# Output projection moved into the head loop, and V 30 and V 31 loaded in smaller pieces

## The chip, the cores and the metric

One core of a Trainium2 chip runs the whole program. The metric is the device time of one execution in microseconds (us); a profiled execution also gives a span, from the first to the last instruction, which is about 2 us shorter (1292.4 against 1294.16 us in the profiled execution of the kernel before). A time is the median of several executions; a profile shows one of them.

Engines: in this kernel PE does matmuls, DVE and ACT do vector and scalar work, POOL a few small things, SP issues nearly all DMA transfers. The DMA share on the profile's page is a mean over the core's 16 DMA engines. SBUF and PSUM are the core's on-chip memories; this kernel has PE write its results to PSUM. A load is counted as landed at the 16th increment of its semaphore. The granted clock is the share of PE's full clock that the profile records as granted; in the records it is 0.5 or 1.

## The reference, cut to what matters

One decode step of an attention block and an MLP. The caches are 32 heads x 32768 keys x 128 in bf16: 268 MB of K and 268 MB of V, each byte used once.

```python
def _A_ref(x, k_cache, v_cache, wq, wo):          # B = Sq = 1, D = 512, H = 32, Sk = 32768, Dh = 128
    q = (x @ wq).reshape(B, Sq, H, Dh).transpose(0, 2, 1, 3)
    scores = jnp.einsum("bhqd,bhkd->bhqk", q, k_cache) * (Dh ** -0.5)
    p = softmax(scores)
    o = jnp.einsum("bhqk,bhkd->bhqd", p, v_cache)
    return o.transpose(0, 2, 1, 3).reshape(B, Sq, H * Dh) @ wo
h  = x + _A_ref(layernorm(x), ...)
h2 = h + mish_mlp(layernorm(h))                   # 512 -> 1376 -> 512
```

## The kernel before

A head is 32 groups of 1024 keys. In each group PE transposes K into PSUM (`tps`), DVE copies the result to SBUF (`kt`), PE forms scores (`sps`), and PE forms the V product (`ops`) of a group 40 groups back. V 31 is the V of head 31, K 31 its K. PE runs heads 2 to 31 as a hardware loop; all other engines run straight-line code. K and V use two halves of one ring; V 31, the last V, goes into the K half.

Each load is one DMA issued by SP in a fixed order (`pos`), after what it overwrites was used (`after`). A normal load is half a head, 4 MB, with 32 KB per partition; 128 in the list below means 4 MB, and 32 means 1 MB (8 KB per partition).

```python
LAST_K = [128, 32, 32, 32, 32]
LAST_V = [128, 64, 32, 16, 8, 8]
# ...
for j, n in enumerate(sizes):
    g1 = g + n // 8
    if kind == "k":
        after = [f"trb{(h - 1) * GH + g1 - 1}"] if h else []
        pos, count = h * GH + g, h
    else:
        after = [f"pv{(h - 1) * GH + g1 - 1}"] if h else ...
        if own:                                   # V 31
            after = [f"trb{h * GH + g1 - 1}"]
        pos, count = (h + 1) * GH + LAG + g + 0.5, h + 1
# ...
```

The output projection runs after the loop, between the groups of the last V product: 31 products of one row, four matmuls (the profile shows 8, L649) that fold the row into columns, and row sums `wbar` of wo.

```python
def y_row(h):
    p = 32 * (h % 4)
    S.step(PE, lambda: t_.matmul(yrow[p:p + 1, :], oT[:, h:h + 1], wo_sb[:, h, :], ...),
           waits=[f"oT{h}", ("wo", 16)], name=f"yr{h}")
# ... after the loop:
for t in range(GH):
    group(H, t)                                   # ends V 30, begins V 31
    if t == 1:
        y_init()
        for h in range(H - 2, H):
            w_bar(h)
        # ...
    if 2 <= t < 8:
        for h in range((H - 2) * (t - 2) // 6, (H - 2) * (t - 1) // 6):
            y_row(h)
    # ...
```

The copy is this one, 1024 times in a run:

```python
def evac(i):
    # ...
    dve(i, lambda: v.tensor_copy(kt[:, i % NE, :], T_b[i % 2][:, :]), f"ev{i}", waits)
```

Of the kernel before, what the change touches and what calls it, by code (L numbers as in the profile page):

```python
# [19 lines left out]
LAST_K = [128, 32, 32, 32, 32]  # L20
LAST_V = [128, 64, 32, 16, 8, 8]

# [10 lines left out]
class _Sched:  # L33
# [5 lines left out]
    def __init__(self, nc, emit, events, sems, only=None):  # L39
        self.nc = nc  # L40
        self.emit = emit
        self.only = only
        self.ev = events
        self.sems = sems
        self.cnt = {}
        self.waited = {}
        self.taken = {}
        self.skip = False
        self.log = []
        self.engines = None  # L50
        if emit:
            self.engines = {PE: nc.tensor, ACT: nc.scalar, DVE: nc.vector, POOL: nc.gpsimd, SP: nc.sync}
# [66 lines left out]
    def repeat(self, rounds, body):  # L119

        if not self.emit or self.only != PE:
            for r in rounds:
                body(r)
            return
        first = None
        for r in rounds:
            self.waited, self.log = {}, []
            if r == rounds[0]:
                with self.nc.Fori(0, len(rounds), 1, engines=[mybir.EngineType.PE],
                                  head_slot={mybir.EngineType.PE: 0}):  # L130
                    body(r)
                first = self.log
                self.skip = True
            else:
                body(r)
                assert self.log == first, r
        self.skip = False
        self.waited = {}
# [27 lines left out]
def plan_loads(H, GH):  # L166


    NH = GH * 8 // PIECE
    loads = []  # L170
    for h in range(H):
        for kind in "kv":
            own = h == 0 if kind == "k" else h == H - 1
            sizes = (FIRST_K if kind == "k" else LAST_V) if own else [PIECE] * NH
            if kind == "k" and h == H - 1:
                sizes = LAST_K
            assert sum(sizes) == GH * 8 and max(sizes) <= PIECE
            g = 0
# [6 lines that stand above are left out]
                    after = [f"pv{(h - 1) * GH + g1 - 1}"] if h else ["q_done"] if g1 > GH // 2 else []  # L185
                    if own:
                        after = [f"trb{h * GH + g1 - 1}"]
                    pos, count = (h + 1) * GH + LAG + g + 0.5, h + 1
                chan = f"{kind}own{j}" if own else f"{kind}{j}"
                if kind == "k" and h == H - 1 and j >= NH - 1:  # L190
                    after = after + ["kx_off"]
                if j >= NH and not own:
                    chan, count = f"kx{j - NH}", 1
                loads.append(_Load(kind, h, g, g1, pos, chan, 16 if own else 16 * count, after))
                g = g1
    loads.sort(key=lambda x: x.pos)
    return loads


def build_kernel(nc, A_x, A_k_cache, A_v_cache, A_wq, A_wo, B_w1, B_b1, B_w2, out, NE=4):  # L200
# [33 lines left out]
    ring = sb([128, 2 * GH * R * 128], BF16, "ring")  # L234
    wo_sb = sb([128, H, D], BF16, "wo_sb")
    w1v = sb([128, KC, F], BF16, "w1_sb")
# [17 lines left out]
    qT = sb([128, 32], BF16, "qT")  # L254
    oT = sb([128, 32], BF16, "oT")
    qcur = sb([128, 2], BF16, "qcur")
    nb = sb([128, 1], F32, "nbias")
# [10 lines left out]
    yrs = sb([128, D], F32, "yrs")  # L268
    pscr = sb([1, 1], F32, "pscr")
    FP = FJ + FJ % 2  # L270
# [19 lines left out]
    Q0 = 160  # L290
    YC = yps[:, 0:KC * WIDE:WIDE]
    HROW = 128
# [43 lines left out]
    def program(S):  # L336
# [54 lines left out]
        for x in range(NX):  # L391
            S.dma(POOL, lambda x=x: g_.sem_inc(sems[f"kx{x}"], 16))

# [7 lines left out]
            b1r[FJ - 1:FJ, 0:FLAST], B_b1[(FJ - 1) * 128:F].rearrange("(o m) -> o m", o=1)).then_inc(sems["b1"], 16))  # L401
        for x in range(NX):
            S.dma(POOL, lambda x=x: g_.sem_inc(sems[f"kx{x}"], -16), waits=[f"trb{NK - GH - 1}"])
        S.step(POOL, lambda: g_.memset(pscr[:, :], 0.0), name="kx_off")
        S.step(DVE, lambda: v.memset(onesm[:, :], 1.0 / D))
# [4 lines left out]
        S.step(DVE, lambda: v.memset(onesf[:, :], 1.0))  # L410
        S.step(DVE, lambda: v.memset(yps[:, :], 0.0))
        S.step(DVE, lambda: v.memset(yrow[:, :], 0.0), name="consts")

# [82 lines left out]
        def values(i):  # L496
# [8 lines left out]
            if ld:  # L505
                waits.append((ld.chan, ld.count))
                if h < H - 1:
                    take[1] = (ld.chan, 16)
            for r in range(R):
                c = g * R + r  # L510
# [5 lines left out]
        def y_cols(h):  # L516
            waits = [f"oT{h}", ("wo", 16)]
            for c in range(KC):
                S.step(PE, lambda c=c: t_.matmul(
                    yps[:, c * WIDE:(c + 1) * WIDE], wo_sb[:, h, c * 128:(c + 1) * 128],  # L520
                    oT[:, h:h + 1].to_broadcast([128, WIDE]),
                    start=False, stop=(h == H - 1), skip_group_check=True), waits=(waits if c == 0 else ()),
                    name=(f"yc{h}" if c == KC - 1 else None))

        def y_row(h):
            p = 32 * (h % 4)
            S.step(PE, lambda: t_.matmul(  # L527
                yrow[p:p + 1, :], oT[:, h:h + 1], wo_sb[:, h, :], start=(h < 4), stop=(h >= H - 5),
                skip_group_check=True), waits=[f"oT{h}", ("wo", 16)], name=f"yr{h}")

        def y_init():
            for c in range(KC):
                S.step(PE, lambda c=c: t_.matmul(
                    yps[:, c * WIDE:(c + 1) * WIDE], xrow[0:1, c * 128:(c + 1) * 128],
                    oneb[0:1, 0:1].to_broadcast([1, WIDE]),
                    start=(c == 0), stop=False, skip_group_check=True),
                    waits=(["consts", ("xr", 16)] if c == 0 else ()))

# [3 lines left out]
        def group(hk, t):  # L542
# [52 lines left out]
            if 0 <= ho < H:  # L595
                if t == 2:
                    S.step(DVE, lambda: v.tensor_scalar_mul(o1s[:, ho:ho + 1], o_b[0][:, 0:1], rtot[:, ho:ho + 1]),  # L597
                           name=f"o1s{ho}", waits=[f"pv{ho * GH + GH - LAG - 1}", f"rcp{ho}"])
                elif t == LAG + 1:
                    add_o(ho)  # L600
                elif t == GH // 2 + 8 and ho < H - 2:
                    w_bar(ho)

        def add_o(ho):
            dve(LAG + 1, lambda: v.scalar_tensor_tensor(  # L605
                oT[:, ho:ho + 1], o_b[1][:, 0:1], rtot[:, ho:ho + 1], o1s[:, ho:ho + 1], ALU.mult, ALU.add),
                f"oT{ho}", [f"pv{ho * GH + GH - 1}", f"o1s{ho}"])

# [8 lines left out]
        def whole(hk):  # L617
            for t in range(GH):
                group(hk, t)

        S.repeat(range(2, H), whole)


        hl = H - 1
        for t in range(GH):
            group(H, t)
            if t == 1:
                y_init()
                for h in range(H - 2, H):
# [5 lines left out]
                    waits=["wbh0"])  # L635
            if 2 <= t < 8:
                for h in range((H - 2) * (t - 2) // 6, (H - 2) * (t - 1) // 6):
                    y_row(h)
            if t == LAG + 2:
                y_row(H - 2)  # L640
                S.step(DVE, lambda: v.tensor_tensor(wbo[:, 0:hl], wbar[:, 0:hl], oT[:, 0:hl], ALU.mult), name="wbo",
                       waits=[f"yr{H - 2}"])
                S.step(DVE, lambda: v.tensor_reduce(wbs[:, :], wbo[:, 0:hl], AXX, ALU.add), name="wbs", waits=["wbo"])
                S.step(DVE, lambda: v.tensor_copy(yrs[:, :], yrow[:, :]), name="yrs")
            if t == LAG + 6:
                S.step(PE, lambda: t_.matmul(YM, onesm[:, :], wbs[:, :], start=False, stop=False, skip_group_check=True),
                       waits=["wbs"])
                for c in range(KC):
                    S.step(PE, lambda c=c: t_.matmul(  # L649
                        yps[:, c * WIDE:c * WIDE + 1], yrs[:, c * 128:(c + 1) * 128], onesf[:, 0:1],  # L650
                        start=False, stop=False, skip_group_check=True), waits=(["yrs"] if c == 0 else ()))
                S.step(PE, lambda: t_.matmul(T_b[0][:, 0:FP], b1r[:, :], identb[0:FP, 0:FP],
# [104 lines left out]
```

## Time and profile before

| | before |
|---|---|
| time, median of the 3 runs | 1295.8 us |
| span of the profiled execution | 1292.4 us |
| last K piece lands | 1263.14 us |
| last V piece lands | 1282.88 us |
| V product ends (PE) | 1284.02 us |
| output copy starts | 1289.97 us |

The landings are read from the trace's semaphore records. These lines are from the profile's page of the kernel before: busy time per engine, the busy tenths of the DMA engines and their GB/s in 40 slices of the span, and the DMA queues (packets, MB, share of 16 engines' span).

```profile
PE 1028.1 (80%) x25114; PEld 994.3 (77%) x25114; DVE 776.2 (60%) x1379; ACT 34.0 (3%) x134; POOL 2.6 (0%) x11
...
DMA  9999999999999999999999999999999999999997
GB/s 373 424 411 425 430 431 429 436 430 430 433 428 435 433 428 433 428 435 433 428 435 429 432 434 427 432 433 429 433 431 430 426 427 434 427 434 428 431 405 285
...
q1 hardware_dynamic: 27816, 548.09, 99.4%
q8 instruction: 20, 0.33, 0.1%
q14 instruction: 13, 0.11, 0.0%
```

The mean over the 16 DMA engines is at 9 tenths or more up to the last slice.

The chain of waits of the kernel before, its end (start us, us, what; followed back from the last instruction):

```profile
1277.72 4.81 PE ops L511 x181
1282.52 0.86 issue
1283.38 0.65 PE ops L511 x19
...
1284.06 0.23 DVE oT L605
...
1285.24 0.73 PE sps L676 x24
1285.98 0.22 PE hlp L683 x2
1286.20 0.73 PE sps L676 x20
...
1288.58 1.37 PE yps L707 x44
...
1289.97 0.29 DVE outsb L711
```

PE works through the groups of V 31 without a wait for data and ends 1.14 us after the last landing. PE is behind here, not DMA; the 0.86 us called issue is a stall in the middle of a group, where no wait stands. The last instruction fetch before it (16 KB, on the queue q8) began at 1280.82 us and took 1.05 us.

Two lines of the timeline before (start us, us, engine, line, operation, count, and the idle time before it with what ended it):

```profile
1260.70 0.36 PE L511 MATMUL ops<-pbuf,ring 128*128 128x32 bf16 x8 [3.10 <-DMA ring<-in_A_v_cache_dram]
...
1283.38 0.64 PE L511 MATMUL ops<-pbuf,ring 128*128 128x32 bf16 x19 [0.86 <-issue]
```

The first is PE's wait for the second half of V 30, 3.1 us.

### The profile page before, as it was taken

How to read it: one execution, taken by the hardware profiler on the slowest of the kernel's cores; microseconds unless marked ns; L12 is line 12 of the kernel's file. 1: busy time of each engine (PE TensorE's matmuls, PEld its weight loads, DVE VectorE, ACT ScalarE, POOL GpSimd, SP SyncE). 2: the span in 40 equal slices, each digit the busy share in tenths (PEclk: the TensorE clock that was granted, in tenths of full speed). 3: DMA queues.
4: the chain of work that ended last, by engine and by line, in shares of the span. 5: the costliest groups of instructions: out<-in, count | busy, mean ns of one | idle time of the engine just before them, and what ended most of it. 6: DMA issues, size and time to landing. Idle time of an engine off the chain costs nothing.

```text
span 1292.4 us, 52224 instructions
## 1 busy us (share of the span) xinstructions
PE 1028.1 (80%) x25114; PEld 994.3 (77%) x25114; DVE 776.2 (60%) x1379; ACT 34.0 (3%) x134; POOL 2.6 (0%) x11
## 2 busy tenths in 40 slices
PE   6757877787787788787787787887877877878888
PEld 6757877787787787787787777887877877877876
DVE  5635566565666565565565665665655655655663
ACT  0000000000000000000000000000000000000000
POOL 0000000000000000000000000000000000000000
PEclk9868888998988998988998988988998888988988
DMA  9999999999999999999999999999999999999997
GB/s 373 424 411 425 430 431 429 436 430 430 433 428 435 433 428 433 428 435 433 428 435 429 432 434 427 432 433 429 433 431 430 426 427 434 427 434 428 431 405 285
DMA packets 27945, 548.53 MB, mean 424 GB/s; under 512 B 2600, under 2 KB 9608, under 8 KB 10888
## 3 DMA queue, kind: packets, MB, share of 16 engines
q1 hardware_dynamic: 27816, 548.09, 99.4%
q8 instruction: 20, 0.33, 0.1%
q14 instruction: 13, 0.11, 0.0%
q0 software_dynamic: 96, 0.00, 0.0%
HBM read 548.08 MB, written 0.00 MB: 424 GB/s over the span
## 4 chain that ended last, share of the span: by engine, by line
DMA 63%; PE 33%; DVE 3%; issue 0%; SPq 0%; ACT 0%
DMA ring<-in_A_k_cache_dram 50%; PE tps L470 17%; DMA ring<-in_A_v_cache_dram 14%; PE ops L511 7%; PE sps L491 6%; DVE kt L479 1%; PE hlp L581 1%; DVE scb L563 1%; DVE pmax L561 1%; PE hlp L565 1%; PE hlp L569 1%; PE yrow L527 0%; SPq L352 0%; PE sps L676 0%; PE yps L707 0%
## 5 line engine op out<-in xcount | busy, mean ns | idle before, releaser
L479 DVE COPY kt<-tps 128x1024 bf16<-128x1024 bf16 x1024 | 707.5, 692 | 487.2 <-PE tps L470 480.1
L470 PE MATMUL tps<-identb,ring 128*128 128x128 bf16 x8192 | 695.8, 234 | 192.7 <-DMA ring<-in_A_k_cache_dram 191.5
L470 PEld LDWEIGHTS tps<-identb,ring 128*128 128x128 bf16 x8192 | 523.3, 104 | 199.7 <-DMA ring<-in_A_k_cache_dram 198.5
L511 PE MATMUL ops<-pbuf,ring 128*128 128x32 bf16 x8192 | 361.2, 178 | 51.6 <-DMA ring<-in_A_v_cache_dram 50.3
L491 PE MATMUL sps<-qcur,kt 128*128 128x32 bf16 x8192 | 376.0, 180 | 8.2 <-DVE scb L563 6.8
L491 PEld LDWEIGHTS sps<-qcur,kt 128*128 128x128 bf16 x8192 | 328.7, 99 | 16.2 <-DVE scb L563 14.4
L511 PEld LDWEIGHTS ops<-pbuf,ring 128*128 128x128 bf16 x8192 | 281.3, 97 | 65.8 <-DMA ring<-in_A_v_cache_dram 50.1
L572 ACT ACTIVATE pbuf<-scb,nbias 128x192 bf16<-128x192 f32 x32 | 14.6, 456 | 1174.5 <-PE ops L511 1100.1
L610 DVE TENSOR_REDUCE wbar<-wo_sb 128x1 f32<-128x512 bf16 x32 | 21.6, 676 | 0.0
L581 PE MATMUL hlp<-esum,onesf 128*128 128x1 f32 x128 | 18.7, 250 | 0.0
L581 PEld LDWEIGHTS hlp<-esum,onesf 128*128 128x128 f32 x128 | 16.7, 190 | 0.2 <-issue 0.2
L561 DVE TENSOR_REDUCE pmax<-sps 128x1 f32<-128x256 f32 x32 | 13.3, 415 | 0.5 <-PE sps L491 0.5
L563 DVE COPY scb<-sps 128x256 f32<-128x256 f32 x32 | 13.2, 414 | 0.0
L565 PE MATMUL hlp<-ident,pmax 128*1 128x128 f32 x64 | 13.1, 290 | 0.0
L576 ACT ACTIVATE pbuf<-scb,nbias 128x64 bf16<-128x64 f32 x32 | 11.2, 348 | 62.1 <-PE ops L511 62.1
L569 PE MATMUL hlp<-gmax,onesr 1*128 1x1 f32 x64 | 12.1, 256 | 0.5 <-DVE gmax L567 0.5
L569 PEld LDWEIGHTS hlp<-gmax,onesr 1*128 1x128 f32 x64 | 9.4, 182 | 2.0 <-DVE gmax L567 1.0
L605 DVE SCALAR_TENSOR_TENSOR oT<-ops,rtot,o1s 128x1 bf16<-128x1 f32 x32 | 6.8, 212 | 5.1 <-PE ops L511 5.1
L597 DVE TENSOR_SCALAR o1s<-ops,rtot 128x1 f32<-128x1 f32 x32 | 6.7, 209 | 3.4 <-PE ops L511 3.4
L567 DVE TENSOR_REDUCE gmax<-hlp 1x1 f32<-1x128 f32 x32 | 8.7, 271 | 0.1
L576 ACT ACTIVATION_READ_ACCUMULATOR pbuf<-scb,nbias 128x1 f32 x32 | 6.0, 187 | 0.0
L572 ACT ACTIVATION_READ_ACCUMULATOR pbuf<-scb,nbias 128x1 f32 x32 | 6.0, 186 | 0.0
(87 smaller groups left out, 60.1 us busy)
## 6 DMA issues: line engine op xcount, KB each, us to landing
ring<-in_A_v_cache_dram SPq DMA_DIRECT2D x63, 4096.0 KB, 20.9
ring<-in_A_k_cache_dram SPq DMA_DIRECT2D x62, 4096.0 KB, 23.1
ring<-in_A_k_cache_dram SPq DMA_DIRECT2D x5, 1024.0 KB, 17.6
wo_sb<-in_A_wo_dram SPq DMA_DIRECT2D x1, 4096.0 KB, 37.7
ring<-in_A_wq_dram SPq DMA_DIRECT2D x1, 3584.0 KB, 30.6
ring<-in_A_k_cache_dram SPq DMA_DIRECT2D x1, 2048.0 KB, 12.3
ring<-in_A_v_cache_dram SPq DMA_DIRECT2D x1, 2048.0 KB, 21.2
ring<-in_A_v_cache_dram SPq DMA_DIRECT2D x1, 1024.0 KB, 17.1
```

The costliest lines, as they stand in the source:

```text
L470: S.step(PE, lambda r=r: t_.matmul(tb[:, r * 128:(r + 1) * 128], block("k", i, r), identb[:, :], is_transpose=True, start=True, stop=True) ...
L479: dve(i, lambda: v.tensor_copy(kt[:, i % NE, :], T_b[i % 2][:, :]), f"ev{i}", waits)
L491: S.step(PE, lambda r=r, c=c: t_.matmul(S_b[:, c:c + WIDE], kt[:, i % NE, r * 128:(r + 1) * 128], q.to_broadcast([128, WIDE]), start=True, ...
L511: S.step(PE, lambda r=r, c=c: t_.matmul(ob[:, 0:WIDE], block("v", i, r), pbuf[:, c:c + 1].to_broadcast([128, WIDE]), start=(r == 0 and g i ...
L561: dve(i, lambda: v.tensor_reduce(pmax[:, :], S_b[:, 0:NCOL], AXX, ALU.max), f"pmax{hs}", [f"qkb{hs * GH + GH - 1}"])
L563: dve(i, lambda: v.tensor_copy(scb[:, :], S_b[:, 0:NCOL]), f"sc{hs}", [])
L565: S.step(PE, lambda: t_.matmul(A_REG, pmax[:, :], ident[:, :], start=True, stop=True), name=f"A{hs}", waits=[f"pmax{hs}"] + (["qT" if H > ...
L569: S.step(PE, lambda: t_.matmul(B_REG, onesr[0:1, :], gmax[0:1, :], start=True, stop=True), name=f"B{hs}", waits=[f"gmax{hs}"])
L572: S.step(ACT, lambda: a.activation(pbuf[:, 0:CV], scb[:, 0:CV], ACTF.Exp, bias=nb[:, :], scale=SC, accum_out=esum[:, 0:1]), name=f"exp{hs} ...
L576: S.step(ACT, lambda: a.activation(pbuf[:, CV:NCOL], scb[:, CV:NCOL], ACTF.Exp, bias=nb[:, :], scale=SC, accum_out=esum[:, 1:2]), name=f"e ...
L581: S.step(PE, lambda s=s: t_.matmul(C_REG, onesf[:, :], esum[:, s:s + 1], start=(s == 0), stop=(s == 1)), name=(f"C{hs}" if s else None), w ...
L610: S.step(DVE, lambda: v.tensor_reduce(wbar[:, h:h + 1], wo_sb[:, h, :], AXX, ALU.add), waits=[("wo", 16)], name=f"wbar{h}")
```

## The change

The intent: take PE work out of the tail (the projection's row products go into the loop, one per head, with wo addressed by the loop's register), and let PE begin V 30's second half and V 31's first half earlier, by loading them in 1 MB pieces. Because PE's loop has one code for all heads, the extra V pieces get semaphores `vx` that stand at 16 in all other heads, as `kx` already did for K 31.

```diff
-LAST_V = [128, 64, 32, 16, 8, 8]
+LAST_V = [32, 32, 32, 32, 64, 32, 16, 8, 8]
...
-            if kind == "k" and h == H - 1:
+            if (kind, h) in (("k", H - 1), ("v", H - 2)):
                 sizes = LAST_K
...
-                if kind == "k" and h == H - 1 and j >= NH - 1:
-                    after = after + ["kx_off"]
+                if (kind, h) in (("k", H - 1), ("v", H - 2)) and j >= NH - 1:
+                    after = after + [f"{kind}x_off"]
...
         def y_row(h):
-            p = 32 * (h % 4)
+            rhs = wo_sb[:, h, :] if S.round is None else wo_flat[:, bass.ds(S.round * D, D)]
             S.step(PE, lambda: t_.matmul(
-                yrow[p:p + 1, :], oT[:, h:h + 1], wo_sb[:, h, :], start=(h < 4), stop=(h >= H - 5),
-                skip_group_check=True), waits=[f"oT{h}", ("wo", 16)], name=f"yr{h}")
+                yrow[:, :], ocur[:, 0:1].to_broadcast([128, 128]), rhs, start=False, stop=(h == H - 2),
+                skip_group_check=True), waits=[f"oc{h}"], name=f"yr{h}")
...
                 elif t == LAG + 1:
+                    if ho < H - 1:
+                        dve(LAG + 1, lambda: v.scalar_tensor_tensor(
+                            ocur[:, :], o_b[1][:, 0:1], rtot[:, ho:ho + 1], o1s[:, ho:ho + 1], ALU.mult, ALU.add), ...)
                     add_o(ho)
+                elif t == LAG + 4 and ho < H - 1:
+                    y_row(ho)
...
-            if 2 <= t < 8:
-                for h in range((H - 2) * (t - 2) // 6, (H - 2) * (t - 1) // 6):
-                    y_row(h)
...
-                for c in range(KC):                      # fold the row into columns by 4 matmuls
-                    ...
+                for c in range(KC):                      # or: mask with the identity on DVE, reduce, 1 matmul
+                    S.step(DVE, lambda c=c: v.tensor_tensor(
+                        yrs[:, c * 128:(c + 1) * 128], yrow[:, c * 128:(c + 1) * 128], ident[:, :], ALU.mult), ...)
...
```

The row sums of wo for heads 30 and 31 also move, from t = 1 (in front of the last softmax on DVE) to t = LAG.

More of the change, by code (lines that the diff above doesn't have):

```diff
@@ L49, in __init__ @@
         self.log = []
+        self.round = None
         self.engines = None
@@ L129, in repeat @@
                 with self.nc.Fori(0, len(rounds), 1, engines=[mybir.EngineType.PE],
-                                  head_slot={mybir.EngineType.PE: 0}):
+                                  head_slot={mybir.EngineType.PE: 0}) as i:
+                    self.round = i
                     body(r)
                 first = self.log
+                self.round = None
                 self.skip = True
@@ L189, in plan_loads @@
                 chan = f"{kind}own{j}" if own else f"{kind}{j}"
-                if kind == "k" and h == H - 1 and j >= NH - 1:
-                    after = after + ["kx_off"]
+                if (kind, h) in (("k", H - 1), ("v", H - 2)) and j >= NH - 1:
+                    after = after + [f"{kind}x_off"]
                 if j >= NH and not own:
-                    chan, count = f"kx{j - NH}", 1
+                    chan, count = f"{kind}x{j - NH}", 1
                 loads.append(_Load(kind, h, g, g1, pos, chan, 16 if own else 16 * count, after))
@@ L234, in build_kernel @@
     ring = sb([128, 2 * GH * R * 128], BF16, "ring")
-    wo_sb = sb([128, H, D], BF16, "wo_sb")
+    wo_flat = sb([128, H * D], BF16, "wo_sb")
+    wo_sb = wo_flat.rearrange("p (h n) -> p h n", h=H)
     w1v = sb([128, KC, F], BF16, "w1_sb")
@@ L255, in build_kernel @@
     oT = sb([128, 32], BF16, "oT")
+    ocur = sb([128, 1], BF16, "ocur")
     qcur = sb([128, 2], BF16, "qcur")
@@ L268, in build_kernel @@
     yrs = sb([128, D], F32, "yrs")
-    pscr = sb([1, 1], F32, "pscr")
+    ycol = sb([128, KC], F32, "ycol")
+    pscr = sb([1, 2], F32, "pscr")
     FP = FJ + FJ % 2
@@ L290, in build_kernel @@
     Q0 = 160
-    YC = yps[:, 0:KC * WIDE:WIDE]
+    YC = yps[:, 0:KC]
     HROW = 128
@@ L391, in program @@
         for x in range(NX):
-            S.dma(POOL, lambda x=x: g_.sem_inc(sems[f"kx{x}"], 16))
+            for k in "kv":
+                S.dma(POOL, lambda x=x, k=k: g_.sem_inc(sems[f"{k}x{x}"], 16))
         S.step(POOL, lambda: g_.iota(identi[:, :], [[-1, 128]], base=0, channel_multiplier=1), name="iota")
@@ L401, in program @@
             b1r[FJ - 1:FJ, 0:FLAST], B_b1[(FJ - 1) * 128:F].rearrange("(o m) -> o m", o=1)).then_inc(sems["b1"], 16))
-        for x in range(NX):
-            S.dma(POOL, lambda x=x: g_.sem_inc(sems[f"kx{x}"], -16), waits=[f"trb{NK - GH - 1}"])
-        S.step(POOL, lambda: g_.memset(pscr[:, :], 0.0), name="kx_off")
+        for k, done in (("k", f"trb{NK - GH - 1}"), ("v", f"pv{NK - 2 * GH - 1}")):
+            for x in range(NX):
+                S.dma(POOL, lambda x=x, k=k: g_.sem_inc(sems[f"{k}x{x}"], -16), waits=[done])
+            S.step(POOL, lambda: g_.memset(pscr[:, "kv".index(k):"kv".index(k) + 1], 0.0), name=f"{k}x_off")
         S.step(DVE, lambda: v.memset(onesm[:, :], 1.0 / D))
@@ L410, in program @@
         S.step(DVE, lambda: v.memset(onesf[:, :], 1.0))
-        S.step(DVE, lambda: v.memset(yps[:, :], 0.0))
-        S.step(DVE, lambda: v.memset(yrow[:, :], 0.0), name="consts")
+        S.step(DVE, lambda: v.memset(yps[:, :], 0.0), name="consts")
         S.step(ACT, lambda: a.preload_act_table_set("natural_log_exp_and_others"), count=False)
@@ L505, in values @@
             if ld:
-                waits.append((ld.chan, ld.count))
-                if h < H - 1:
+                if ld.chan[1] != "x":
+                    waits.append((ld.chan, ld.count))
+                if h < H - 1 and ld.chan[1] != "x":
                     take[1] = (ld.chan, 16)
+            if h < H - 1:
+                if g == GH // 2:
+                    for x in range(NX):
+                        take[2 + x] = (f"vx{x}", -16)
+                elif g in XG:
+                    x = XG.index(g)
+                    waits.append((f"vx{x}", 16))
+                    take[1] = (f"vx{x}", 16)
             for r in range(R):
@@ L519, in y_cols @@
                 S.step(PE, lambda c=c: t_.matmul(
-                    yps[:, c * WIDE:(c + 1) * WIDE], wo_sb[:, h, c * 128:(c + 1) * 128],
-                    oT[:, h:h + 1].to_broadcast([128, WIDE]),
+                    yps[:, c:c + 1], wo_sb[:, h, c * 128:(c + 1) * 128], oT[:, h:h + 1],
                     start=False, stop=(h == H - 1), skip_group_check=True), waits=(waits if c == 0 else ()),
@@ L525, in y_row @@
         def y_row(h):
-            p = 32 * (h % 4)
+            rhs = wo_sb[:, h, :] if S.round is None else wo_flat[:, bass.ds(S.round * D, D)]
             S.step(PE, lambda: t_.matmul(
-                yrow[p:p + 1, :], oT[:, h:h + 1], wo_sb[:, h, :], start=(h < 4), stop=(h >= H - 5),
-                skip_group_check=True), waits=[f"oT{h}", ("wo", 16)], name=f"yr{h}")
+                yrow[:, :], ocur[:, 0:1].to_broadcast([128, 128]), rhs, start=False, stop=(h == H - 2),
+                skip_group_check=True), waits=[f"oc{h}"], name=f"yr{h}")
         def y_init():
-            for c in range(KC):
-                S.step(PE, lambda c=c: t_.matmul(
-                    yps[:, c * WIDE:(c + 1) * WIDE], xrow[0:1, c * 128:(c + 1) * 128],
-                    oneb[0:1, 0:1].to_broadcast([1, WIDE]),
-                    start=(c == 0), stop=False, skip_group_check=True),
-                    waits=(["consts", ("xr", 16)] if c == 0 else ()))
+            S.step(PE, lambda: t_.matmul(
+                yrow[:, :], oneb[0:1, 0:1].to_broadcast([1, 128]), xrow[0:1, :], start=True, stop=False,
+                skip_group_check=True), waits=["consts", ("xr", 16), ("wo", 16)])
         CV = (GH - LAG) * R
@@ L599, in group @@
                 elif t == LAG + 1:
+                    if ho < H - 1:
+                        dve(LAG + 1, lambda: v.scalar_tensor_tensor(
+                            ocur[:, :], o_b[1][:, 0:1], rtot[:, ho:ho + 1], o1s[:, ho:ho + 1], ALU.mult, ALU.add),
+                            f"oc{ho}", [f"pv{ho * GH + GH - 1}", f"o1s{ho}"] + ([f"yr{ho - 1}"] if ho else []))
                     add_o(ho)
+                elif t == LAG + 4 and ho < H - 1:
+                    y_row(ho)
                 elif t == GH // 2 + 8 and ho < H - 2:
@@ L604, in add_o @@
         def add_o(ho):
-            dve(LAG + 1, lambda: v.scalar_tensor_tensor(
+            S.step(DVE, lambda: v.scalar_tensor_tensor(
                 oT[:, ho:ho + 1], o_b[1][:, 0:1], rtot[:, ho:ho + 1], o1s[:, ho:ho + 1], ALU.mult, ALU.add),
-                f"oT{ho}", [f"pv{ho * GH + GH - 1}", f"o1s{ho}"])
+                name=f"oT{ho}", waits=[f"pv{ho * GH + GH - 1}", f"o1s{ho}"])
         def w_bar(h):
@@ L619, in whole @@
                 group(hk, t)
+        y_init()
         S.repeat(range(2, H), whole)
@@ L626, in program @@
             group(H, t)
-            if t == 1:
-                y_init()
+            if t == LAG:
                 for h in range(H - 2, H):
@@ L635, in program @@
                     waits=["wbh0"])
-            if 2 <= t < 8:
-                for h in range((H - 2) * (t - 2) // 6, (H - 2) * (t - 1) // 6):
-                    y_row(h)
-            if t == LAG + 2:
-                y_row(H - 2)
+            if t == LAG + 5:
                 S.step(DVE, lambda: v.tensor_tensor(wbo[:, 0:hl], wbar[:, 0:hl], oT[:, 0:hl], ALU.mult), name="wbo",
-                       waits=[f"yr{H - 2}"])
+                       waits=[f"wbar{hl - 1}", f"oT{hl - 1}"])
                 S.step(DVE, lambda: v.tensor_reduce(wbs[:, :], wbo[:, 0:hl], AXX, ALU.add), name="wbs", waits=["wbo"])
-                S.step(DVE, lambda: v.tensor_copy(yrs[:, :], yrow[:, :]), name="yrs")
-            if t == LAG + 6:
+                for c in range(KC):
+                    S.step(DVE, lambda c=c: v.tensor_tensor(
+                        yrs[:, c * 128:(c + 1) * 128], yrow[:, c * 128:(c + 1) * 128], ident[:, :], ALU.mult),
+                        waits=[f"yr{hl - 1}"], name=(f"yrs" if c == KC - 1 else None))
+                S.step(DVE, lambda: v.tensor_reduce(
+                    ycol[:, :], yrs[:, :].rearrange("p (c n) -> p c n", c=KC), AXX, ALU.add), name="ycol", waits=["yrs"])
+            if t == LAG + 9:
+                S.step(PE, lambda: t_.matmul(YC, ident[:, :], ycol[:, :], start=True, stop=False,
+                                             skip_group_check=True), waits=["ycol"])
                 S.step(PE, lambda: t_.matmul(YM, onesm[:, :], wbs[:, :], start=False, stop=False, skip_group_check=True),
                        waits=["wbs"])
-                for c in range(KC):
-                    S.step(PE, lambda c=c: t_.matmul(
-                        yps[:, c * WIDE:c * WIDE + 1], yrs[:, c * 128:(c + 1) * 128], onesf[:, 0:1],
-                        start=False, stop=False, skip_group_check=True), waits=(["yrs"] if c == 0 else ()))
                 S.step(PE, lambda: t_.matmul(T_b[0][:, 0:FP], b1r[:, :], identb[0:FP, 0:FP],
```

## The prediction

> **What bounds it now.** The DMA queue, from start to the last V piece. The page's slices give a DMA busy share of 9 tenths or more up to the last slice. In the trace's record of loads landing, one 4 MB load lands every 9.71 us (432 GB/s) for the whole loop. [...] PE (80% busy) and DVE (60%) do not bind in the loop.
>
> At the end the landings are still back to back: second half of V 30 at 1260.65 us, last quarter of K 31 at 1263.14, pieces of V 31 at 1272.86, 1277.80, 1280.36, 1281.62, 1282.23, 1282.88. From 1250.95 to 1282.88, 13.6 MB take 31.9 us, against 31.6 at 432 GB/s. So no order of loads can bring the last V in much before 1282.9. The timeline shows what follows: PE ends its V product at 1284.03, the FFN chain ends with the output copy at 1290.26. In the weights' landings, the last w2 piece comes at 1288.62.
>
> **What the change does, costed.**
> - Removes from the tail 31 row products (groups of five take 0.52 us on the chain of waits: about 3.2 us), eight products that fold the row into columns (0.89), and moves two row sums of wo (1.27 on DVE) out of the last softmax. Adds there four masked products, one reduction, two small matmuls. In the loop: one 128x512 matmul and one 0.21 us DVE operation per head, plus a register offset: free, as PE has slack there.
> - V 30's second half as four 1 MB pieces: all four wait for the same event as the one load did (V 29 finished, 1242.97 us) plus a POOL step. But the first now lands about 1253.4 instead of 1260.65, and K 31's last quarter about 1255.8 instead of 1263.14. That removes PE's 3.1 us wait at 1257.6 (timeline), and K 31 ends about 3 us earlier. Pieces of 1 MB cost nothing: K 31's land 2.43 us apart, 432 GB/s.
> - V 31's first half in quarters lands its first rows about 7 us earlier, the last at the same time.
>
> So PE gets ahead in the tail, but then waits for V 31's last pieces. **On the critical path** remains only what PE was behind at the end: 1284.03 minus (1282.88 + one last group of 8 matmuls, 0.21, plus about 0.1 latency), i.e. 0.8 us. Part of that 0.8 is the 0.86 us stall of PE at 1282.52, which the profile calls issue and which follows an instruction fetch; it may fall elsewhere in the new tail.
>
> **Prediction.** The span falls by about 0.8 us, from 1292.4 to 1291.6; time 1294.9 us, range 1293.2 to 1296.6. Chances: faster by over 2% 0.01, within 2% 0.98, slower by over 2% 0.01.
>
> **What would show it.** Right: last V landing still near 1282.9; no PE wait of 3 us for V 30; PE gaps for V in the last 10 us; V product ended about 0.3 us after the last landing; loads still 9.71 us apart in the loop. Wrong: the last V lands over 1 us earlier or later, or PE is still working off a backlog then.
>
> **What would make it wrong.** About every 118 us one load takes some 1 us longer (10.7 instead of 9.7), mostly beside a small instruction fetch: one more or fewer moves the result as much as the change. PE, now waiting, may run the last chain at the lower granted clock (0.50 occurs after waits). The 0.86 us fetch stall may land inside the FFN chain. More pieces may cost some 0.05 us each.

The sum: 1284.03 - 1282.88 - 0.21 - 0.1 = 0.84, so 0.8 us. The 0.1 us of latency is the author's estimate; the trace of before has 0.05 us from a landing (1260.65) to the first matmul that uses it (1260.70). The 0.05 us per piece is an estimate too: K 31's last piece took 2.49 us against 2.43. "0.50 occurs after waits" can be seen in the clock record of before: in the 3.41 us before each of its 62 falls to 0.50, PE is busy 32% of the time in the median, against 80% over the run.

## More of the kernel before

The two queues named instruction move 0.44 MB of 548.

## The result, and the profile after

Ratios here and below are the mean time of one kernel's runs over that of the other's in the same rounds, so not quite the ratio of the medians.

| | before | after |
|---|---|---|
| time, median (4 runs each) | 1295.1 us | 1294.39 us |
| ratio to before, 95% interval | | 0.9994 (0.9976 to 1.0011) |
| span of the profiled execution | 1292.4 us | 1292.5 us |
| last K piece lands | 1263.14 us | 1255.91 us |
| last V piece lands | 1282.88 us | 1283.46 us |
| V product ends | 1284.02 us | 1283.91 us |
| output copy starts | 1289.97 us | 1290.15 us |

The page of the kernel after, the same lines:

```profile
PE 1030.9 (80%) x25105; PEld 995.3 (77%) x25105; DVE 777.5 (60%) x1413; ACT 33.9 (3%) x134; POOL 2.7 (0%) x12
...
DMA  9999999999999999999999999999999999999997
GB/s 373 424 410 423 434 432 428 435 430 430 436 427 434 431 431 433 428 434 432 430 433 429 432 434 429 433 429 424 431 431 430 435 427 434 432 430 428 431 382 305
...
q1 hardware_dynamic: 28680, 548.09, 99.3%
q8 instruction: 20, 0.33, 0.1%
q14 instruction: 13, 0.11, 0.0%
```

The chain of waits after, its end:

```profile
1264.62 18.84 DMA ring<-in_A_v_cache_dram
1283.46 0.05 issue
1283.51 0.41 PE ops L527 x8
...
1283.94 0.23 DVE oT L625
...
1285.15 0.78 PE sps L696 x24
1285.93 0.43 PE hlp L703 x2
1286.36 0.76 PE sps L696 x20
...
1288.76 1.37 PE yps L727 x44
...
1290.15 0.29 DVE outsb L731
```

And PE's waits in the timeline after:

```profile
1278.27 1.89 PE L527 MATMUL ops<-pbuf,ring 128*128 128x32 bf16 x64 [3.92 <-DMA ring<-in_A_v_cache_dram]
...
1280.76 1.04 PE L527 MATMUL ops<-pbuf,ring 128*128 128x32 bf16 x32 [0.59 <-DMA ring<-in_A_v_cache_dram]
...
1282.04 1.10 PE L527 MATMUL ops<-pbuf,ring 128*128 128x32 bf16 x24 [0.24 <-DMA ring<-in_A_v_cache_dram]
...
1283.51 0.40 PE L527 MATMUL ops<-pbuf,ring 128*128 128x32 bf16 x8 [0.37 <-DMA ring<-in_A_v_cache_dram]
```

The change did to PE what it was meant to do. The 3.1 us wait for V 30 is gone, K 31 is done earlier, and PE catches up so well that it idles 3.9 us at 1274 and then waits before nearly every piece. In the chain, the end of the program now hangs on one DMA, the last piece of V 31, in place of PE's backlog. The last landing did not come earlier. It came 0.58 us later.

Term by term, of the profiled executions: last landing +0.58 us; from there to the start of `oT`, 1.17 before and 0.48 after, -0.69; from `oT` to the output copy, 5.91 before and 6.21 after, +0.30. The sum is +0.19 us, the difference of the spans. This holds for two single executions. The profiled one of the kernel before (1294.16 us) is among its quicker ones: its 25 other runs lie between 1293.63 and 1297.37 us, with a median of 1295.21, while the four of the kernel after lie between 1294.19 and 1294.85. What happens in the slower runs of before, no trace shows.

The last term fits PE's clock. These lines give busy time per engine, granted clock, DMA share and GB/s from 1280 to 1285 us, first of the kernel before:

```profile
1280.00:1285.00 5.00, 3.46 (x120) 3.17 (x116) 0.72 (x4) 0.00 (x0) 0.00 (x0) 0.70 0.65 197
```

and of the kernel after:

```profile
1280.00:1285.00 5.00, 2.93 (x77) 2.32 (x73) 0.83 (x5) 0.00 (x0) 0.00 (x0) 0.50 0.95 305
```

PE gets half the clock throughout this stretch after the change (0.50), and 0.70 on average before it. The two chains above tell where the 0.30 us go: the steps of DVE and ACT take as long as before to 0.02 us, and the growth lies in PE's steps. The two matmuls of `hlp` take 0.22 us in the kernel before, where the clock record has full speed from 1283.05 to 1286.46 us, and 0.43 in the kernel after, at half speed. In act_half_proj, one of the runs below, full speed lasts from 1280.10 to 1283.51 us; `hlp` falls inside it and takes 0.22 us again, and the chain from `oT` to the copy takes 5.82.

Why the clock falls is another matter. In 60 of the 62 falls in the kernel before, PE is busy 52% or less of the 3.41 us before the fall (3.41 us is the shortest stretch in the clock record). The other two are in the tail, and little work just before does not explain the fall there: in the kernel before it fell at 1279.64 us, after 3.41 us in which the profile has PE busy throughout (and again at 1286.46, after 64%). In the kernel after, the clock fell at 1273.86 us, before PE's wait of 3.92 us began at 1274.36, with PE busy 2.49 us of the 3.41 before. The cause of the fall stays open.

### The profile page after: what moved, and what is told of

Read it like the earlier page. It is cut to its first block, busy times and chain, and to the rows that moved or that the text cites. A ratio compares the mean times of both kernels' runs of the same rounds, so it can differ in the third digit from the quotient of the medians.

```text
span 1292.5 us, 52344 instructions
## 1 busy us (share of the span) xinstructions
PE 1030.9 (80%) x25105; PEld 995.3 (77%) x25105; DVE 777.5 (60%) x1413; ACT 33.9 (3%) x134; POOL 2.7 (0%) x12
## 4 chain that ended last, share of the span: by engine, by line
DMA 59%; PE 37%; DVE 3%; issue 0%; SPq 0%; ACT 0%
DMA ring<-in_A_k_cache_dram 53%; PE tps L477 19%; PE ops L527 7%; PE sps L498 7%; DMA ring<-in_A_v_cache_dram 6%; DVE kt L486 1%; PE hlp L595 1%; PE hlp L579 1%; DVE scb L577 1%; DVE pmax L575 1%; PE hlp L583 1%; PE yrow L544 1%; SPq L358 0%; PE sps L696 0%; PE yps L727 0%
## 5 line engine op out<-in xcount | busy, mean ns | idle before, releaser
L544 PE MATMUL yrow<-wo_sb,ocur 128*128 (+1 forms) x31 | 11.7, 376 | 0.0
L615 DVE SCALAR_TENSOR_TENSOR ocur<-ops,rtot,o1s 128x1 bf16<-128x1 f32 x31 | 6.6, 212 | 0.0
```

The source lines that it names most:

```text
L544: S.step(PE, lambda: t_.matmul(yrow[:, :], ocur[:, 0:1].to_broadcast([128, 128]), rhs, start=False, stop=(h == H - 2), skip_group_check=Tr ...
```

## A second look at the landings: one engine of 16 is late

Why does the last V land at 1283 at all? A load of K or V raises its semaphore 16 times in both traces. What they stand for can be read from the packet records of the kernel before. V 31's last two pieces are 256 packets of 2 KB. 240 of them had ended by 1278.23 us; the last 16 ended one after another, 0.08 us apart, from 1281.15 to 1282.35, and the last increment came at 1282.88, 0.53 us after them. The last increment but one, at 1278.77, came 0.54 us after the last of the 240. So an increment follows the end of one chain of packets. A chain is taken here as the work of one of the 16 DMA engines; this is inferred, as the packets carry no engine number. Read so, the 16 increments of one load, sorted, show how far the engines are apart. From the traces, in us before the last increment:

```text
before, V 31's last piece, landed 1282.88:
-6.04 -6.01 -5.95 -5.92 -5.87 -5.86 -5.84 -5.82 -5.79 -5.71 -5.67 -5.63 -5.47 -5.40 -4.11  0.00
after,  V 31's last piece, landed 1283.46:
-4.93 -4.82 -4.81 -4.78 -4.78 -4.76 -4.73 -4.72 -4.59 -4.59 -4.55 -4.54 -4.51 -4.46 -3.10  0.00
```

Fifteen engines are done more than 3 us, most of them 4.5 to 6 us, before the sixteenth. The page's DMA share, a mean over 16, does not show it. The lag grows during the run in steps. Two loads before and after one step, in the kernel before:

```text
landed  295.15: -4.99 -4.95 -4.87 -4.84 -4.81 -4.63 -3.99 -2.66 -1.72 -1.70 -1.64 -1.57 -1.56 -1.48 -0.84 0.00
   8 KB instruction fetch on q14 at 295.67
landed  304.86: -5.00 -4.96 -4.87 -4.84 -4.81 -4.63 -3.98 -1.71 -1.69 -1.68 -1.65 -1.57 -1.56 -1.49 -0.83 0.00

landed 1007.58: -7.51 -7.35 -7.34 -7.33 -7.31 -7.00 -6.44 -5.07 -5.02 -4.89 -4.88 -4.75 -4.67 -4.04 -3.21 0.00
   8 KB instruction fetch on q14 at 1009.51
landed 1018.23: -8.46 -8.29 -8.29 -8.24 -8.24 -7.91 -7.38 -6.01 -5.96 -5.83 -5.81 -5.70 -5.62 -4.99 -4.16 0.00
```

In the first pair one engine, 2.66 us ahead of the last, loses 0.95 us; nothing is seen in the landing. In the second pair all the others move 0.95 us ahead at once, which means that the last one lost 0.95 us itself, and the load lands 10.65 us after the one before instead of 9.71. These are the losses of 1 us that the prediction had noticed about every 118 us. It had not asked what they were.

Theory F: each fetch of 8 KB of DVE instructions (128 instructions, so 64 bytes each, as dve_double below shows: 1024 instructions more, 8 fetches more; DVE runs 42 per head, a head takes 38.9 us, so one fetch about every 118 us) holds one and the same DMA engine back by 0.95 us. That engine starts ahead of the slowest, passes it near 540 us, and from then on sets every landing, the last one too. Theory S is its consequence for this change: work of PE in the tail hardly counts, because it ends on the straggler's last piece. The rivals: P, the tail of PE sets the time; R, the losses come from the memory or the clock, not from fetches. Why a fetch whose transfer takes 0.33 us costs the engine 0.95 us, no run shows.

## The experiments

The profiled executions of all of them are in one table at the end. Ten kernels were run, four times each, except dve_double, act_double and probe_engines, which ran twice. act_half_pieces and act_20_of_32 ran on another chip than the other eight; ratios are always to runs of the kernel before in the same job.

### Each half of the change alone

**proj_only.** The kernel after, with the loads of before.

```diff
-LAST_V = [32, 32, 32, 32, 64, 32, 16, 8, 8]
+LAST_V = [128, 64, 32, 16, 8, 8]
-            if (kind, h) in (("k", H - 1), ("v", H - 2)):
+            if (kind, h) in (("k", H - 1),):
...            # and no vx semaphores
```

> The new output projection with the old loads. Theory S (the last V piece is held back by one lagging DMA engine out of 16, so work of PE in the tail does not count): last V lands at 1282.9 us +-0.4 as before, the V product ends 0.2 to 0.5 us later instead of 1.15, span 1291.4 to 1292.2, ratio to before 0.999 to 1.000. Rival P (PE's backlog in the tail sets the time): the 3 to 4 us of row products and row sums taken out of the tail come off the span, 1288 to 1289.5, ratio 0.997.

The end of its chain of waits:

```profile
1282.90 0.38 PE ops L519 x8
...
1283.30 0.23 DVE oT L617
...
1289.45 0.29 DVE outsb L723
```

Measured: span 1291.8 us, ratio 0.9986 (0.9969 to 1.0003). The last V lands at 1282.85 and the V product ends 0.41 us later instead of 1.14. So the projection alone gives the 0.7 us that PE was behind, and not the 3 to 4 us that were taken out of the tail. Rival P falls by the spans: those of all four runs are 1291.7 to 1292.0, and it asked for 1288 to 1289.5. The times alone would not refute it, as their interval holds its 0.997 and also 1. That there is a gain of 0.7 is read from the profile; the slower chain after `oT` (6.15 us against 5.91) takes 0.24 of it back.

**pieces_only.** The kernel before, with the loads of after.

```diff
-LAST_V = [128, 64, 32, 16, 8, 8]
+LAST_V = [32, 32, 32, 32, 64, 32, 16, 8, 8]
-            if kind == "k" and h == H - 1:
+            if (kind, h) in (("k", H - 1), ("v", H - 2)):
...            # and the vx semaphores of the change
```

> The new loads with the old projection. Theory S: PE's 3 us wait for V 30 is gone and K 31 ends about 3 us earlier, but the last V lands at 1283.4 +-0.4, some 0.5 us later than before, because pieces of 8 KB rows move 1.8% slower per byte (0.309 us for 8 KB against 1.2135 us for 32 KB in the traces); span 1292.0 to 1293.0, ratio 1.000. Rival P: PE's backlog shrinks by 3 us and the span falls to about 1289.5.

Measured: span 1293.0 us, ratio 0.9993 (0.9976 to 1.0009). PE's 3 us wait for V 30 is gone, the V product ends 0.44 us after the last landing, and the last V lands at 1283.93, a little over the expected window. Nothing is gained.

What do the pieces cost? From the landing of K 31's third small piece to that of the last V, the bytes are the same in all kernels. The five kernels with the old loads (leaving out the failed probe below) take 31.93, 32.07, 32.31, 32.22 and 32.00 us for it, the four with the new loads 32.53, 32.72, 32.64 and 32.60; the two kernels with tiny instructions added, below, also have the new loads and take 32.41 and 32.44. The means are 32.11 and 32.56: the pieces cost some 0.45 us. A transfer of 8 KB to one partition took 0.309 us in the trace and one of 32 KB 1.2135 to 1.216 us, so the small rows are 1.6 to 1.9% slower per byte, which over the 8 MB now in such rows explains 0.3 to 0.35 us of it, by estimate. By these times the 1 MB pieces reach 98% of the rate of the 4 MB loads.

### More instructions on DVE, and on ACT

**dve_double.** The kernel after with one more tiny instruction on DVE per group.

```diff
             dve(i, lambda: v.tensor_copy(kt[:, i % NE, :], T_b[i % 2][:, :]), f"ev{i}", waits)
+            S.step(DVE, lambda: v.memset(scr[0:1, i:i + 1], 0.0), count=False)
```

> The kernel after, with one more tiny DVE instruction (a memset of one element) per group of K, 1024 in all. DVE stays under 70% busy. Theory F: fetches of 8 KB for DVE rise from 11 to 19, each holds the same DMA engine back by about 0.95 us, so the losses of 1 us between landings double in number and the span grows by 6 to 8.5 us, to 1298.5 to 1301. Rival R (losses come from the memory at fixed times, or from PE): losses stay about 118 us apart, span within 1 us of 1292.5.

**act_double.** The control: as many tiny instructions on ACT.

```diff
+            S.step(ACT, lambda: a.activation(scr[0:1, i:i + 1], onesr[0:1, 0:1], ACTF.Copy),
+                   waits=[f"trb{i}", "consts"], count=False)
```

> Control: the kernel after with 1024 tiny instructions added on ACT instead of DVE. The same bytes of instructions more are fetched. Theory F says that they go to another DMA engine, which starts several us ahead of the slowest, so the span stays within 1 us of 1292.5 and the losses stay about 116 us apart. If any fetch costs, wherever it lands (rival: fetches cost bandwidth as such), the span grows by 6 to 8 us as with DVE.

The queue lines of dve_double; those of act_double have the same q14 line:

```profile
q8 instruction: 20, 0.33, 0.1%
q14 instruction: 21, 0.17, 0.0%
```

Busy time of dve_double:

```profile
PE 1028.4 (79%) x25074; PEld 993.6 (76%) x25105; DVE 780.7 (60%) x2437; ACT 34.0 (3%) x134; POOL 2.7 (0%) x12
```

Measured for dve_double: span 1301.2 us, 8.6 us more than after (1292.5), a little over the expected window (8 fetches of 0.95 us make 7.6; the other 1.0 us is not explained); ratio to before 1.0067 (1.0047 to 1.0087). DVE is busy only 3.2 us more in the whole run. There are 8 more fetches of 8 KB, 1024 instructions divided by 128, and the losses between landings come every 67 us instead of every 118: ten from 540 us to the last K loads, against five.

Measured for act_double: also 8 more fetches, span 1292.3 us, ratio 0.9996 (0.9976 to 1.0016). Nothing is lost, and the losses stay about 117 us apart. So it is not the bytes fetched, nor fetching as such (the same 8 fetches: 8.6 us more for DVE's, 0.2 us less for ACT's), but, by theory F, fetching on the engine that is already last. Theory F holds and rival R falls. In the kernel before, two fetches on q14 stand outside DVE's rhythm of 118 us, at 490.28 and 678.15 us, and are taken for ACT's. Around each of them one early increment comes later, 4.11 in place of 4.80 us and 4.45 in place of 5.18 us before the last one, and the loads still land 9.72 and 9.71 us after the ones before. So what they hold back has over 4 us to spare.

### Half of DVE's copies on ACT

ACT is busy 3% of the time. If half of the K copies go there, DVE runs about 850 instructions instead of 1379 and should fetch less often (11 times before, 7 times measured below), and by theory F ACT's fetches hold back an engine that has several us to spare (over 4 us in the kernel before, see above).

```diff
-            dve(i, lambda: v.tensor_copy(kt[:, i % NE, :], T_b[i % 2][:, :]), f"ev{i}", waits)
+            if i % 2:
+                S.step(ACT, lambda: a.activation(kt[:, i % NE, :], T_b[i % 2][:, :], ACTF.Copy), name=f"ev{i}",
+                       waits=waits, priv=f"{(i % GH) * 2 // GH}{PRIV}")
+            else:
+                dve(i, lambda: v.tensor_copy(kt[:, i % NE, :], T_b[i % 2][:, :]), f"ev{i}", waits)
-    DVE_ROUND = (GH // 2 + 4, GH // 2)
+    DVE_ROUND = (GH // 4 + 4, GH // 4)
                 take[2] = (f"{DVE}{half}{PRIV}", DVE_ROUND[half])
+                take[4] = (f"{ACT}{half}{PRIV}", GH // 4)      # PE's loop counts ACT's copies too
```

This was run on all four corners of the change.

**act_half_before** (old projection, old loads):

> The kernel before, with every second copy of transposed K moved from DVE to ACT, so that DVE runs about 850 instructions instead of 1379. Theory F (each 8 KB fetch of DVE instructions holds one and the same DMA engine back by about 0.95 us, and that engine's lag sets every landing from 540 us on): DVE fetches fall from 11 to 6 or 7, ACT gets 4 or 5 on another engine, loads that take 10.7 us fall from 6 to 2 or less after 500 us, last V lands 3 to 5 us earlier (1278 to 1280), span 1288 to 1290, ratio 0.997. Rival R (the 1 us losses come from the memory, not from fetches): still one loss about each 118 us, span unchanged within 1 us or longer if ACT's copy is slower.

**act_half_after** (the whole change):

> The kernel after with the same move of every second K copy to ACT. Theory F: last V lands 3 to 5 us earlier than 1283.5, span 1287.5 to 1289.5, ratio to before 0.996 to 0.998; now 0 to 1 us faster than the kernel before with the same move, as the floor is lower and PE's backlog counts more. Rival R: unchanged within 1 us.

**act_half_proj** (new projection, old loads):

> New projection, old loads, and every second K copy on ACT. Tells what the smaller pieces are worth once the floor is lower. If pieces only cost (8 KB rows 1.8% slower, some 0.5 us at the end): last V lands at about 1279.1 and the span is 1288.0 to 1288.6, 0.3 to 0.6 us under the variant with pieces (1288.7). If PE needs the early rows: PE's wait for V 30 leaves a backlog, as in the kernel before with the same move (V product ended 2.5 us after the last landing), and the span is 1289 to 1291.

**act_half_pieces** (old projection, new loads):

> The fourth corner: old projection, new loads, every second K copy on ACT. With the copies split, the old projection with old loads had its V product end 2.5 us after the last landing, 2.0 us of it in one stall behind an instruction fetch (span 1290.9); the new projection had none (1288.5). If the early rows of V 30 and V 31 take the backlog away as well as the new projection does: V product ended 0.5 us after the last landing, span 1288.5 to 1289.5. If the projection's 3 us of PE work in the tail still count: 1290 to 1291.

The two engines' copies in act_half_proj (count, then busy us and mean ns of one, then idle before and its releaser):

```profile
L488 ACT ACTIVATE kt<-tps 128x1024 bf16<-128x1024 bf16 x512 | 524.3, 1024 | 674.8 <-PE tps L478 674.8
...
L491 DVE COPY kt<-tps 128x1024 bf16<-128x1024 bf16 x512 | 354.0, 691 | 745.2 <-PE tps L478 744.8
```

ACT's copy takes 1024 ns against 691. It does not matter, as both engines wait for PE most of the time.

Measured: the last V lands at 1279.83, 1279.62, 1279.83 and 1279.65 us in the four kernels, 3.0 to 4.3 us earlier than in the same kernels without the move. No byte of K or V was taken away. The losses from 540 us on fall from five or six to two or three (act_half_before has three, where two or fewer were expected). DVE's fetches of 8 KB, told apart by their spacing of 193 us, fall from 11 to 7. In act_half_proj the last V was expected at 1279.1; it landed 0.2 us later than with the pieces, because K 31's third piece was already 0.63 us later. So this pair alone does not show what the pieces cost.

The spans are 1290.9, 1288.7, 1288.5 and 1288.7. The kernel before gains least, and the reason is in its chain of waits (act_half_before):

```profile
1274.79 4.82 PE ops L516 x181
1279.61 2.01 issue
1281.62 0.66 PE ops L516 x19
...
1282.30 0.23 DVE oT L610
```

Now the data are there at 1279.83, and PE is not: the stall that cost 0.86 us stands at the same place, 19 matmuls from the end, and lasts 2.01 us. The last fetch on q8 before it began at 1279.07 and ended at 1280.19; in the kernel before, at 1280.82 and 1281.87. In both, PE goes on 1.4 to 1.5 us after the fetch ended. That PE waits there for its next instructions is inferred from this, not seen. For that reason act_half_before missed its expected span (1288 to 1290). A third case is in act_20_of_32, below: a stall of 0.41 us ends 1.50 us after a 16 KB fetch.

In the profiles with PE's work taken out of the tail, or with the rows there early, this stall is gone. So on the lowered floor the change is worth 2.2 us of span in the profiles, 2.4 us with the projection alone and 2.1 with the pieces alone. By the medians of the times it is 2.0, 2.3 and 1.4: two of the four runs of act_half_pieces have spans of 1289.7 and 1290.0, over 1 us more than its profiled one. That the pieces alone remove the stall in every run is not shown. The ratios to the kernel before are 0.9979 (0.9963 to 0.9996), 0.9964 (0.9947 to 0.9981), 0.9967 (0.9950 to 0.9983) and 0.9969 (0.9953 to 0.9986) in the order above; the intervals overlap, so the differences among the four rest on the profiles. The expectation of 0 to 1 us for act_half_after against act_half_before was too low.

**act_20_of_32.** New projection, old loads, and 20 of 32 copies on ACT, so that DVE and ACT run about as many instructions.

```diff
+        def on_act(t):
+            return t % 2 == 1 or t in (12, 18, 22, 28)
-            if i % 2:
+            if on_act(i % GH):
```

> New projection, old loads, and 20 of 32 K copies on ACT instead of 16: DVE and ACT run about 22 and 24 instructions per head. Theory F: DVE's fetches fall from 7 to about 6 in the run, ACT's rise from 5 to 6; at most one of three visible losses goes, span 1287.3 to 1288.5. If ACT's longer copy (1.02 us against 0.69) begins to hold PE back, losses of more than 1 us appear in PE's waits for ACT and the span is above 1289.

Measured: span 1287.5 us, median 1289.39 us, ratio 0.9955 (0.9938 to 0.9972). DVE and ACT fetch six times each, one loss of 1 us is left after 540 us where act_half_proj had three (at most one was expected to go), and the last V lands at 1277.94. PE waited for ACT's copies 2.2 us in the whole run. Its chain of waits:

```profile
1262.85 15.09 DMA ring<-in_A_v_cache_dram
...
1277.98 0.38 PE ops L527 x8
...
1278.39 0.23 DVE oT L625
...
1279.57 0.46 PE sps L696 x12
1280.03 0.41 issue
1280.44 0.46 PE sps L696 x12
...
1285.12 0.29 DVE outsb L731
```

A stall of this kind, 0.41 us, now stands in the MLP that follows the attention, as the prediction had feared; the 16 KB fetch before it ended at 1278.94. This version still beats both kernels. Against before it gains 0.45%, with an interval that leaves out 1; its four runs (1289.35 to 1289.65) lie under all four of the kernel after (1294.19 to 1294.85), though on another chip and in another job.

### A probe that failed: cutting loads by partitions

**probe_engines.** To learn which engine is late, and to take load off it, the first three loads of V 31 were cut by partitions, so that the larger part should use fewer engines. (The trace shows what came of it: after the increments at issue, the three cut loads raise their semaphores 23, 16 and 24 times, where an uncut load has 16 increments. This fits 15 + 8, 14 + 2 and 13 + 11.)

```diff
+CUT = {0: 120, 16: 126, 24: 117}
...
-            S.dma(SP, lambda: sp.dma_start(dst, src).then_inc(sems[ld.chan], 16), waits=ld.after)
+                S.dma(SP, lambda: sp.dma_start(dst[0:cut], src[0:cut]).then_inc(sems[ld.chan], 16), waits=ld.after)
+                S.dma(SP, lambda: sp.dma_start(dst[cut:128], src[cut:128]).then_inc(sems[ld.chan], 16))
```

> New projection, old loads, but the first three loads of V 31 are cut by partitions into 120+8, 126+2 and 117+11[...]. Which engine lags is unknown. If it is the last one, the 120-partition load comes without a straggler: its increments of the semaphore end within 2 us of each other, the lagging engine catches up by 9.7 us, and the last V lands 3 to 5 us earlier (1278 to 1280), span 1287.5 to 1289. If it is the 15th or 14th, the same from the second or the third load on, with less gain. If it is a lower one, nothing is gained and the span is up to 1.5 us longer than that of the projection alone (1291.8).

Measured: span 1318.7 us, ratio 1.0206 (1.0186 to 1.0227), 27 us slower, far outside every expected window. The DMA engines are as busy as ever and in the end move less than half. Two stretches of probe_engines, with DMA share and GB/s last:

```profile
1250.00:1260.00 10.00, 7.88 (x226) 7.78 (x222) 7.50 (x11) 0.00 (x0) 0.00 (x0) 1.00 1.05 367
...
1270.00:1280.00 10.00, 7.13 (x176) 6.57 (x173) 5.84 (x15) 0.99 (x4) 0.00 (x0) 0.72 0.96 157
```

Even V 30's second half, issued uncut just before, took 13.0 us to land after the load before it instead of 9.7. Why, no run here shows. Which engine is late stays open, and this is not a cheap way to relieve it.

### All runs in one table

Figures of the profiled executions, in us; losses are loads that land over 10.2 us after the one before, from 540 us to 1232 us.

| kernel | median | last K lands | last V lands | V product ends | span | losses |
|---|---|---|---|---|---|---|
| before | 1295.1 | 1263.14 | 1282.88 | 1284.02 | 1292.4 | 5 |
| after | 1294.39 | 1255.91 | 1283.46 | 1283.91 | 1292.5 | 5 |
| proj_only | 1293.64 | 1262.98 | 1282.85 | 1283.26 | 1291.8 | 6 |
| pieces_only | 1294.61 | 1256.18 | 1283.93 | 1284.37 | 1293.0 | 5 |
| dve_double | 1303.47 | 1264.67 | 1292.11 | 1292.55 | 1301.2 | 10 |
| act_double | 1294.35 | 1255.72 | 1283.21 | 1283.65 | 1292.3 | 6 |
| act_half_before | 1292.69 | 1259.74 | 1279.83 | 1282.26 | 1290.9 | 3 |
| act_half_after | 1290.68 | 1251.96 | 1279.62 | 1280.06 | 1288.7 | 3 |
| act_half_proj | 1290.44 | 1259.82 | 1279.83 | 1280.26 | 1288.5 | 3 |
| act_half_pieces | 1291.31 | 1252.03 | 1279.65 | 1280.09 | 1288.7 | 2 |
| act_20_of_32 | 1289.39 | 1258.16 | 1277.94 | 1278.35 | 1287.5 | 1 |
| probe_engines | 1321.53 | 1269.54 | 1309.58 | 1310.02 | 1318.7 | 6 |

## Why the prediction was right or wrong

- **Within 2%, and the time, 1294.9 with a range of 1293.2 to 1296.6:** right; 1294.39 was measured. This is a weak test, as the range also holds the time of the kernel before, 1295.1. The span was predicted to fall by 0.8 us to 1291.6, and in the profiles it rose by 0.19, to 1292.5. The reason given, that a tail bound by the last landing takes little from PE's head start, is shown by proj_only and pieces_only: both remove PE's delay, and the span of the one is 0.5 us shorter than before, that of the other 0.6 us longer.
- **"0.8 us" on the critical path:** right for the term. From the last landing to `oT`, 0.69 us were saved. Of the estimated 0.3 us that must remain, 0.45 was measured.
- **PE's waits:** right. The 3.1 us wait went, and waits of 3.9, 0.6, 0.2 and 0.4 us for V 31 came.
- **"Pieces of 1 MB cost nothing: K 31's land 2.43 us apart":** wrong in size. They cost some 0.45 us over the tail (eleven kernels). Two intervals of K 31 were taken as the rule; K 31's last small piece, in the same trace, took 2.49. The prediction's list of what could go wrong had 0.05 us per piece, which makes 0.3 us for six more pieces, but the sum did not use it.
- **The lower clock of the last chain:** listed as a risk, and it came: the granted clock was 0.50 and the chain took 0.30 us more, all of it in PE's steps. That it comes after waits fits 60 of the 62 falls in the kernel before, but not this one: the clock fell at 1273.86 us, before PE's long wait began at 1274.36. With the later last landing, most of it from the pieces, this ate the 0.7 us gained. proj_only shows the same slower chain (6.15 us from `oT` to the copy), so it is not the pieces that cause it.
- **"So no order of loads can bring the last V in much before 1282.9":** the figure stands for the order, but the floor under it was misread. It was taken for the rate of all DMA engines. It is the rate of one, held back by instruction fetches (0.95 us for each of 8 KB), while fifteen were done 4.11 us or more earlier in the kernel before. With the same loads and the same bytes, moving 20 of 32 copies to ACT brought the last V to 1277.94. The prediction saw the losses "mostly beside a small instruction fetch" and counted them as noise, when fewer of them moved the last landing by 4.9 us.
- **"The loop has PE slack", so that the projection there is free:** right. Outside the losses, loads keep landing 9.71 us apart.

## What to carry to other kernels

When a kernel is bound by DMA, look at the 16 increments of a load and not only at the mean share: here the load was there with the last increment, 4.11 us after the fifteenth in the kernel before, under a mean share of 9 tenths or more up to the last slice. Straight-line instructions are traffic too (0.11 of 548 MB on q14 here); what counted here is which engine their fetches hold back (8.6 us for 8 more fetches on DVE, nothing for 8 more on ACT), so it can pay to spread instruction count over the compute engines even when none of them is busy: with 20 of 32 copies on ACT the last V landed 4.9 us earlier than in proj_only (1277.94 against 1282.85). And work removed behind a floor showed its worth only when the floor moved: the same change was worth 2.2 us of span in the profiles (2.0 us by the medians) once the late engine had been relieved.
